# A light convolution and SwiGLU kernel: the first pair's weight conversion, fetch and loads put in another order

## The chip, the cores and the metric

The kernel runs on one core of one Trainium2 chip. The metric is the device time of one execution in microseconds (us). A few words recur: PE is TensorE, DVE is VectorE, ACT is ScalarE, POOL is GpSimd, SP is SyncE; in the traces read here VectorE, ScalarE, GpSimd and SyncE take their instructions in the order of the program, so a waiting instruction holds up all that stand behind it on its engine.

## The reference

The reference is a causal 7-tap convolution over the sequence with softmaxed taps for each of 8 heads, then a SwiGLU feed-forward with an RMS norm in front of it:

```python
def _moe_ref(x, w_gate, w_val, w_out, rms_g):          # x: 32768 x 192, d_ff 1536
    rms = np.sqrt(np.mean(x * x, axis=-1, keepdims=True) + 1e-06)
    xn = x / rms * rms_g
    g = xn @ w_gate
    silu = g * (1.0 / (1.0 + np.exp(-g)))
    val = xn @ w_val
    return (silu * val @ w_out).astype(np.float32)
```

The weights arrive as 64-bit floats and are turned into fp32 on the chip with integer operations. That conversion is what much of the change is about.

## The kernel before

The tokens are taken in 32 "pairs" of 1024. The d_ff dimension is cut into four "units". From the second pair on, a unit uses sums of weights (a fast matrix product); the first pair runs "plain" units straight from the converted weights, because the sums aren't there yet. The whole opening is a hand-made schedule: generators are stepped at fixed places, and each engine's queue gets its instructions in that order. The parts that matter (cuts marked):

```python
def convert(t, exp, mf, dst, gain=None):
    lo, hi = t[:, :, :, 0], t[:, :, :, 1]          # the two words of a 64-bit float
    nc.vector.tensor_scalar(out=exp, in0=hi, scalar1=20, ...)        # exponent field
    nc.vector.tensor_scalar(out=exp, in0=exp, scalar1=896.0, ...)    # clamp
    yield
    nc.vector.tensor_scalar(out=exp, in0=exp, scalar1=896.0, scalar2=2.0**23, op0=ALU.subtract, op1=ALU.mult)
    nc.vector.tensor_scalar(out=man, in0=hi, scalar1=0xFFFFF, ...)   # mantissa
    yield
    nc.scalar.activation(mf, man, AF.Copy, scale=2.0**-20, bias=1.0)
    # ... then DVE sign (L196), low word (L206) and gain (L211) for input weights;
    #     ACT low word, DVE sign, POOL add and product for output weights

def plain(u, side):
    ht = big.tile([P, 2, NF, T], F32, name="ht")
    n = 0
    for g in (1, 0):
        for f in range(NF):                        # six groups a unit
            bk = free[n % 4]                       # which of four pairs of PSUM banks
            n += 1
            # ... KP x 2 matmuls into bank(0, bk) and bank(1, bk)
            sg = sgs.tile([P, T], F32, name="sg")
            nc.scalar.activation(out=sg[:], in_=bank(0, bk)[:], func=AF.Silu)
            nc.vector.tensor_tensor(out=ht[:, g, f, :], in0=bank(1, bk)[:], in1=sg[:], op=ALU.mult)
            side(n)                                # everything else is stepped here

done(conv(0, True))
# ... norm, conversion of unit 0's weights, transposes
fetch(0, nc.scalar)                                # first x blocks: SyncE and ScalarE
done(cin)
load_in(2, nc.sync)
load_in(3, nc.sync)
cin = convert_in(1)
cout = convert_out()
nxt = front(1)                                     # pair 1: convolution, norm, transposes
step(nxt, 15)
for u in range(NU):
    def side(s):
        step(cin); step(cout); step(nxt, 2); step(ws)
    hts.append(plain(u, side))
    done(ws)
    ws = w_sums(u)                                 # sums of unit u's weights, on GpSimd
    done(cin)
    cin = convert_in(u + 2)
```

I number the groups of the four units 1 to 24 through the whole text; "the product" of a group is VectorE's multiplication of its SiLU and value.

Of the kernel before, what the change touches and what calls it, by code (L numbers as in the profile page):

```python
# [8 lines left out]
AF = mybir.ActivationFunctionType  # L9
ALU = mybir.AluOpType  # L10
AX = mybir.AxisListType
U32 = mybir.dt.uint32
# [3 lines left out]
def kernel(  # L16
# [10 lines left out]
    nc = tc.nc  # L27
# [26 lines left out]
    LOW, UPP = slice(0, HP), slice(HP, P)  # L54
# [66 lines left out]
    def words(w):  # L121
        return w.bitcast(U32).rearrange("r (n two) -> r n two", two=2)

    def load_in(u, q):
        cols = slice(u * NF * P, (u + 1) * NF * P)
        t = big.tile([P, 2, NF, T], F32, name="ht")
        t = t[:].rearrange("p a f t -> p (a f t)")[:, 0 : KP * NF * P * 2].bitcast(U32)
        t = raw["in", u] = t.rearrange("p (k n two) -> p k n two", k=KP, two=2)
        for w, rows in ((moe_w_gate, LOW), (moe_w_val, UPP)):
            for k in range(KP):  # L130
                q.dma_start(out=t[rows, k], in_=words(w)[k * HP : (k + 1) * HP, cols, :])

    def load_out(i, q=nc.gpsimd):
        if i >= NO:
            return
        t = outs.tile([P, T // P, D], F32, name="o_sb")
        t = t[:].rearrange("p j d -> p (j d)").bitcast(U32)
        t = raw["out", i] = t.rearrange("p (f d two) -> p f d two", f=PF, two=2)
        for f in range(PF):
            r = (i * PF + f) * P  # L140
            q.dma_start(out=t[:, f], in_=words(moe_w_out)[r : r + P, :, :])
# [14 lines left out]
        out=taps[:], in0=w_sb[:], in1=stat[:].to_broadcast([P, H, K]), op=ALU.subtract  # L156
# [7 lines left out]
        out=taps[:], in0=taps[:], in1=ssum[:].to_broadcast([P, H, K]), op=ALU.mult  # L164
    )

    def convert(t, exp, mf, dst, gain=None):





        lo, hi = t[:, :, :, 0], t[:, :, :, 1]
        nc.vector.tensor_scalar(  # L174
            out=exp, in0=hi, scalar1=20, scalar2=0x7FF,
            op0=ALU.logical_shift_right, op1=ALU.bitwise_and,
        )
        nc.vector.tensor_scalar(
            out=exp, in0=exp, scalar1=896.0, scalar2=1151.0, op0=ALU.max, op1=ALU.min
        )  # L180
        yield
        nc.vector.tensor_scalar(
            out=exp, in0=exp, scalar1=896.0, scalar2=2.0**23,
            op0=ALU.subtract, op1=ALU.mult,
        )
        man = mf.bitcast(U32)
        nc.vector.tensor_scalar(
            out=man, in0=hi, scalar1=0xFFFFF, scalar2=None, op0=ALU.bitwise_and
        )
        yield  # L190
        nc.scalar.activation(mf, man, AF.Copy, scale=2.0**-20, bias=1.0)
        if gain is None:
            low = lo.bitcast(F32)
            nc.scalar.activation(low, lo, AF.Copy, scale=2.0**-52)
        yield
        nc.vector.scalar_tensor_tensor(  # L196
            out=exp, in0=hi, scalar=0x80000000, in1=exp,
            op0=ALU.bitwise_and, op1=ALU.bitwise_or,
        )
        pw = exp.bitcast(F32)  # L200
        if gain is None:
            nc.gpsimd.tensor_tensor(out=mf, in0=mf, in1=low, op=ALU.add)
            nc.gpsimd.tensor_tensor(out=dst, in0=mf, in1=pw, op=ALU.mult)
        else:
            yield
            nc.vector.scalar_tensor_tensor(  # L206
                out=mf, in0=lo, scalar=2.0**-52, in1=mf, op0=ALU.mult, op1=ALU.add
            )
            yield
            for i in range(dst.shape[1]):  # L210
                nc.vector.scalar_tensor_tensor(  # L211
                    out=dst[:, i, :], in0=mf[:, i, :], scalar=gain[:, i : i + 1],
                    in1=pw[:, i, :], op0=ALU.mult, op1=ALU.mult,
                )
        yield
# [46 lines left out]
    def convert_in(u):  # L262
        if u >= NU:
            return
        dst = wf[u][:, 0:9, :].rearrange("p (k f) n -> p k (f n)", k=KP)
        yield from convert(raw.pop(("in", u)), exp_i[:], mf_i[:], dst, rg_sb)

    def convert_out():
        for i in range(NO):
            dst = wo_sb[:, i * PF : (i + 1) * PF, :]  # L270
            exp_o = cvt.tile([P, PF, D], U32, name="exp_o")
            mf_o = cvt.tile([P, PF, D], F32, name="mf_o")
            yield from convert(raw.pop(("out", i)), exp_o[:], mf_o[:], dst)
            load_out(i + 2)
# [5 lines left out]
    def conv(p, fast=False):  # L280


        if p >= PAIRS:
            return
        t = x_sb.pop(p)
        y = ys[p] = work.tile([P, NJ, D], F32, name="y")
        for k in range(K):
            xk = t[:, k : k + NJ, :]
            if fast and k < 3:
                for h in range(H):  # L290
                    hs = slice(h * GS, (h + 1) * GS)
                    w = taps[:, h, k : k + 1]
                    if k == 0:
                        nc.vector.tensor_scalar(
                            out=y[:, :, hs], in0=xk[:, :, hs], scalar1=w, scalar2=None,
                            op0=ALU.mult,
                        )
                    else:
                        nc.vector.scalar_tensor_tensor(
                            out=y[:, :, hs], in0=xk[:, :, hs], scalar=w, in1=y[:, :, hs],  # L300
                            op0=ALU.mult, op1=ALU.add,
                        )
                yield
                continue
            m = y if k == 0 else prods.tile([P, NJ, D], F32, name="m")
            for h in range(H):
                hs = slice(h * GS, (h + 1) * GS)
                nc.scalar.mul(m[:, :, hs], xk[:, :, hs], taps[:, h, k : k + 1])  # L308
                if h % 2:
                    yield  # L310
            if k > 0:
                nc.vector.tensor_tensor(out=y[:], in0=y[:], in1=m[:], op=ALU.add)  # L312
            yield
        load(p + 1)
# [37 lines left out]
    def place(p):  # L352




        if p >= PAIRS:
            return
        y = ys.pop(p)
        nt = work.tile([P, D // Q, Q, NJ], F32, name="nt")  # L360
        yv = y[:].rearrange("p j (c a) -> p c j a", a=Q)
        nv = nt[:].rearrange("p c b j -> p c j b")
        for c in range(D // Q):
            nc.vector.transpose(out=nv[:, c], in_=yv[:, c])  # L364
            yield
        xd = scr[p] = dram.tile([D, PT], F32, name="xd")
        to = xd[:].rearrange("(c a) (q t) -> q a c t", a=Q, q=NQ)
        for q in range(NQ):
            nc.sync.dma_start(
                out=to[q], in_=nt[q * Q : (q + 1) * Q].rearrange("p c b j -> p c (b j)")  # L370
            )
        yield
# [4 lines left out]
    def blk(i):  # L377
        return xb[:, i // KP, i % KP, :]

    def fetch(p, other=None):  # L380

        if p >= PAIRS:
            return
        xd = scr.pop(p)
        for g in (1, 0):
            for rows, q in ((LOW, nc.sync), (UPP, other or nc.sync)):
                q.dma_start(
                    out=xb[rows, g],
                    in_=xd[:, g * T : (g + 1) * T].rearrange("(k p) t -> p k t", p=HP),
                )  # L390
# [31 lines left out]
    def leftover():  # L422
        while late:
            late.pop()()

    def unit(u, side):


# [44 lines left out]

        mm(9, d, blk(B3), True)
        side(1)
        mm(12, c, cs(SS), True)
        keep("e", c)
# [127 lines left out]
    def step(it, n=1):  # L605
        for _ in range(n):
            next(it, None)

    def done(it):
        for _ in it:  # L610
            pass

    def front(p):
        yield from conv(p)
        yield from norm(p)
        yield from place(p)
# [1 line left out]


    done(conv(0, True))  # L620
    cin = convert_in(0)
    nm = norm(0, True)
    step(nm, 3)
    step(cin, 2)
    done(nm)
    step(cin)
    done(place(0))
    fetch(0, nc.scalar)
    done(cin)
    load_in(2, nc.sync)  # L630
    load_in(3, nc.sync)
    cin = convert_in(1)
    cout = convert_out()
    nxt = front(1)
    step(nxt, 15)
    hts = []
    ws = iter(())
    for u in range(NU):

        def side(s):  # L640
            step(cin)
            step(cout)
            step(nxt, 2)
            step(ws)

        hts.append(plain(u, side))
        done(ws)
        ws = w_sums(u)
        done(cin)
        cin = convert_in(u + 2)  # L650
    done(cout)
    done(nxt)

# [3 lines left out]
    for p in range(PAIRS):  # L657
# [11 lines left out]
        nxt = front(p + 2)  # L669
# [42 lines left out]
```

## Time and profile before

| | before |
|---|---|
| time, median (6 runs beside the changed kernel) | 2848.03 us (2847.11 to 2848.41) |
| TensorE's first matmul | 46.29 us |
| gaps of TensorE before units 1, 2, 3 | 5.25, 4.68, 7.96 us |
| output projection of pair 0 starts | 136.5 us |
| one later pair | 54.94 + 31.32 us of TensorE |

The lines themselves are in the prediction below. In a timeline row come the start in us, the length in us, the engine, the source line, the operation, its output and inputs with their shapes, how many instructions are merged in the row, and in brackets the idle time before it and what ended it. In the page's row of shares each engine has its busy time, its share of the span and its number of instructions.

### The profile page before, as it was taken

How to read it: one execution, taken by the hardware profiler on the slowest of the kernel's cores; microseconds unless marked ns; L12 is line 12 of the kernel's file. 1: busy time of each engine (PE TensorE's matmuls, PEld its weight loads, DVE VectorE, ACT ScalarE, POOL GpSimd, SP SyncE). 2: the span in 40 equal slices, each digit the busy share in tenths (PEclk: the TensorE clock that was granted, in tenths of full speed). 3: DMA queues.
4: the chain of work that ended last, by engine and by line, in shares of the span. 5: the costliest groups of instructions: out<-in, count | busy, mean ns of one | idle time of the engine just before them, and what ended most of it. 6: DMA issues, size and time to landing. Idle time of an engine off the chain costs nothing.

```text
span 2846.6 us, 53025 instructions
## 1 busy us (share of the span) xinstructions
PE 2777.9 (98%) x20512; PEld 2213.8 (78%) x20512; DVE 2095.7 (74%) x3188; ACT 1969.6 (69%) x4743; POOL 470.4 (17%) x409
## 2 busy tenths in 40 slices
PE   2899999999999999999999999999999999999999
PEld 1478887788887788877788877888877888877887
DVE  7677777777777777777777778777777777777754
ACT  5467777677776677776677776777766777766733
POOL 1721111111111111111111111111111111111100
PEclk9899999999999999999999999999999999999999
DMA  6212221112221112212112221122211122121110
GB/s 155 70 42 54 65 59 40 49 48 65 65 54 45 43 54 65 65 40 59 43 54 65 59 46 49 45 61 65 59 40 42 54 65 65 42 57 43 35 45 12
DMA packets 95597, 155.18 MB, mean 55 GB/s; under 512 B 6896, under 2 KB 64752, under 8 KB 91256
## 3 DMA queue, kind: packets, MB, share of 16 engines
q1 hardware_dynamic: 93856, 149.41, 20.4%
q8 instruction: 160, 2.62, 0.4%
q0 software_dynamic: 512, 1.57, 0.2%
q10 hardware_dynamic: 976, 0.82, 0.1%
q14 instruction: 93, 0.76, 0.1%
HBM read 101.44 MB, written 50.33 MB: 53 GB/s over the span
## 4 chain that ended last, share of the span: by engine, by line
PE 97%; DVE 1%; ACT 0%; DMA 0%; issue 0%; SPq 0%; DVEq 0%
PE ps L440 60%; PE ps L563 35%; PE ps L544 2%; DMA xb<-xd 0%; DVE ht L551 0%; DVE nt L364 0%; DVE y L312 0%; DMA xd<-nt 0%; DVE exp_i L196 0%; ACT sq L324 0%; DVE mf_i L206 0%; ACT sg L550 0%; DVE exp_o L174 0%; ACT y L348 0%; DVE o_sb L572 0%
## 5 line engine op out<-in xcount | busy, mean ns | idle before, releaser
L440 PE MATMUL ps<-xc,wf 64*128 64x512 f32 x4960 | 1356.3, 589 | 0.0
L440 PEld LDWEIGHTS ps<-xc,wf 64*128 64x128 f32 x4960 | 782.1, 187 | 327.9 <-issue 12.2
L563 PEld LDWEIGHTS ps<-wo_sb,ht 64*128 64x128 f32 x12288 | 1012.7, 187 | 9.5 <-DVE o_sb L572 4.8
L563 PE MATMUL ps<-wo_sb,ht 64*128 64x192 f32 x12288 | 1017.4, 323 | 0.1
L440 PE MATMUL ps<-xb,wf 64*128 64x512 f32 x2976 | 930.5, 589 | 0.0
L448 ACT COPY tp<-ps 128x512 f32<-128x512 f32 x1240 | 660.0, 588 | 300.8 <-PE ps L440 300.8
L460 ACT ACTIVATE sg<-sg 128x512 f32<-128x512 f32 x744 | 475.8, 639 | 290.0 <-DVE sg L457 290.0
L440 PEld LDWEIGHTS ps<-xb,wf 64*128 64x128 f32 x2976 | 487.6, 187 | 188.3 <-issue 6.4
L457 DVE TENSOR_TENSOR sg<-ps,tp 128x512 f32<-128x512 f32 x620 | 425.1, 686 | 212.0 <-ACT tp L448 210.4
L312 DVE TENSOR_TENSOR y<-y,m 128x1536 f32<-128x1536 f32 x190 | 334.8, 1762 | 298.1 <-ACT m L308 297.7
L308 ACT ACTIVATE m<-x_sb,taps 128x192 f32<-128x192 f32 x1520 | 532.5, 441 | 6.8 <-DMA x_sb<-in_x_dram 6.1
L463 DVE TENSOR_TENSOR ht<-ht,sg 128x512 f32<-128x512 f32 x744 | 484.5, 683 | 0.0
L457 DVE TENSOR_TENSOR ht<-ps,tp 128x512 f32<-128x512 f32 x620 | 422.6, 682 | 0.0
L472 POOL TENSOR_TENSOR tp<-tp,sg 128x512 f32<-128x512 f32 x124 | 179.7, 1449 | 1209.8 <-ACT tp L448 1165.1
L336 POOL TENSOR_SCALAR r<-ss 128x8 f32<-128x8 f32 x32 | 10.5, 327 | 1063.7 <-ACT sq L324 1037.0
L572 DVE TENSOR_TENSOR o_sb<-ps,o_sb 128x192 f32<-128x192 f32 (+1 forms) x192 | 75.7, 420 | 115.5 <-ACT o_sb L571 113.4
L472 POOL TENSOR_TENSOR tp<-tp,ht 128x512 f32<-128x512 f32 x124 | 157.6, 1271 | 0.0
L348 ACT ACTIVATE y<-y,r 128x192 f32<-128x192 f32 x252 | 94.0, 445 | 83.2 <-POOL r L339 83.2
L457 DVE TENSOR_TENSOR sg<-tp,ps 128x512 f32<-128x512 f32 x124 | 85.3, 688 | 85.8 <-ACT tp L448 64.3
L544 PE MATMUL ps<-xb,wf 64*128 64x512 f32 x288 | 72.3, 663 | 64.2 <-DMA xb<-xd 46.3
L571 ACT COPY o_sb<-ps 128x192 f32<-128x192 f32 (+1 forms) x192 | 67.0, 364 | 88.6 <-PE ps L563 88.2
L324 ACT ACTIVATE sq<-y 128x192 f32<-128x192 f32 x252 | 91.6, 363 | 50.5 <-DVE y L312 43.6
(52 smaller groups left out, 779.4 us busy)
## 6 DMA issues: line engine op xcount, KB each, us to landing
xb<-xd SPq DMA_DIRECT2D x126, 384.0 KB, 6.4
x_sb<-in_x_dram SPq DMA_DIRECT2D x24, 1344.0 KB, 5.8
xd<-nt SPq DMA_DIRECT2D x128, 192.0 KB, 3.3
out_dram<-o_sb SPq DMA_DIRECT2D x64, 384.0 KB, 2.6
x_sb<-in_x_dram SPq DMA_DIRECT2D x8, 1176.0 KB, 9.0
ht<-in_moe_w_gate_dram SPq DMA_DIRECT2D x12, 192.0 KB, 9.1
ht<-in_moe_w_val_dram SPq DMA_DIRECT2D x12, 192.0 KB, 5.9
o_sb<-in_moe_w_out_dram POOLq DMA_DIRECT2D x8, 192.0 KB, 2.8
```

The source lines that it names most:

```text
L308: nc.scalar.mul(m[:, :, hs], xk[:, :, hs], taps[:, h, k : k + 1])
L312: nc.vector.tensor_tensor(out=y[:], in0=y[:], in1=m[:], op=ALU.add)
L324: nc.scalar.activation(out=sq[:], in_=y[:, j, :], func=AF.Square, accum_out=ss[:, j : j + 1])
L348: nc.scalar.mul(y[:, j, :], y[:, j, :], r[:, j : j + 1])
L440: nc.tensor.matmul(out=bank(h, bk)[:], lhsT=wf[u][rows, at[i], :], rhs=rhs, start=first, stop=True, skip_group_check=True,)
L448: nc.scalar.copy(out=t[:], in_=bank(h, bk)[:])
L457: nc.vector.tensor_tensor(out=dst, in0=in0, in1=in1, op=op)
L460: nc.scalar.activation(out=og[o][:], in_=og[o][:], func=AF.Silu)
L463: nc.vector.tensor_tensor(out=ov[o], in0=ov[o], in1=og[o][:], op=ALU.mult)
L472: nc.gpsimd.tensor_tensor(out=t[:], in0=sb["a", h][:], in1=o3, op=ALU.add)
L544: nc.tensor.matmul(out=bank(h, bk)[:], lhsT=wf[u][HALF[h], k * NF + f, :], rhs=xb[HALF[h], g, k, :], start=(k == 0), stop=(k == KP - 1), s ...
L563: nc.tensor.matmul(out=bank(h, bk)[:, w : w + D], lhsT=hts[f // NF][HALF[h], g, f % NF, j * P : (j + 1) * P], rhs=wo_sb[HALF[h], f, :], st ...
```

## The change

It means to remove the three gaps of TensorE in the first pair. Five things move: one of VectorE's exponent steps becomes a ScalarE copy; the first fetch of x is issued by SyncE alone, so that ScalarE needn't wait in front of it; the third unit's weights are loaded before the fetch; the second unit's weights are converted before the first unit instead of beside it; and the later conversions are stepped at chosen groups.

```diff
         nc.vector.tensor_scalar(
             out=exp, in0=exp, scalar1=896.0, scalar2=1151.0, op0=ALU.max, op1=ALU.min
         )
-        yield
-        nc.vector.tensor_scalar(
-            out=exp, in0=exp, scalar1=896.0, scalar2=2.0**23,
-            op0=ALU.subtract, op1=ALU.mult,
-        )
 ... (mantissa as before)
         yield
+        nc.scalar.activation(exp, exp, AF.Copy, scale=2.0**23, bias=-896.0 * 2.0**23)
         nc.scalar.activation(mf, man, AF.Copy, scale=2.0**-20, bias=1.0)
 ...
     done(conv(0, True))
-    cin = convert_in(0)
+    load_in(2, nc.sync)
     nm = norm(0, True)
     step(nm, 3)
-    step(cin, 2)
+    cin = convert_in(0)
+    step(cin)
     done(nm)
     step(cin)
     done(place(0))
-    fetch(0, nc.scalar)
+    fetch(0)
+    load_in(3, nc.sync)
+    nxt = front(1)
+    step(nxt, 5)
     done(cin)
-    load_in(2, nc.sync)
-    load_in(3, nc.sync)
     cin = convert_in(1)
+    step(cin)
+    step(nxt, 5)
+    step(cin)
+    step(nxt, 5)
+    done(cin)
 ... (inputs(): convert_in(2), then convert_in(3))
         def side(s):
-            step(cin)
+            n = 6 * u + s
+            if n <= 13 and n % 2 or 14 <= n <= 16:
+                step(cin)
             step(cout)
             step(nxt, 2)
             step(ws)
```

More of the change, by code (lines that the diff above doesn't have):

```diff
@@ L173, in convert @@
         lo, hi = t[:, :, :, 0], t[:, :, :, 1]
+        man = mf.bitcast(U32)
         nc.vector.tensor_scalar(
@@ L180, in convert @@
         )
-        yield
-        nc.vector.tensor_scalar(
-            out=exp, in0=exp, scalar1=896.0, scalar2=2.0**23,
-            op0=ALU.subtract, op1=ALU.mult,
-        )
-        man = mf.bitcast(U32)
         nc.vector.tensor_scalar(
@@ L378, in blk, with fetch @@
         return xb[:, i // KP, i % KP, :]
-    def fetch(p, other=None):
+    def fetch(p):
         if p >= PAIRS:
@@ L385, in fetch @@
         for g in (1, 0):
-            for rows, q in ((LOW, nc.sync), (UPP, other or nc.sync)):
-                q.dma_start(
+            for rows in (LOW, UPP):
+                nc.sync.dma_start(
                     out=xb[rows, g],
@@ L627, with inputs @@
     done(place(0))
-    fetch(0, nc.scalar)
+    fetch(0)
+    load_in(3, nc.sync)
+    nxt = front(1)
+    step(nxt, 5)
     done(cin)
-    load_in(2, nc.sync)
-    load_in(3, nc.sync)
     cin = convert_in(1)
+    step(cin)
[3 more added lines that the diff above has]
+    done(cin)
+    def inputs():
+        yield from convert_in(2)
+        yield from convert_in(3)
+    cin = inputs()
     cout = convert_out()
-    nxt = front(1)
-    step(nxt, 15)
     hts = []
@@ L648 @@
         ws = w_sums(u)
-        done(cin)
-        cin = convert_in(u + 2)
+    done(cin)
     done(cout)
```

## The prediction

> **What bounds the kernel now.** I first read the page's engine shares and its chain that ended last.
>
> ```profile
> PE 2777.9 (98%) x20512; PEld 2213.8 (78%) x20512; DVE 2095.7 (74%) x3188; ACT 1969.6 (69%) x4743; POOL 470.4 (17%) x409
> PE 97%; DVE 1%; ACT 0%; DMA 0%; issue 0%; SPq 0%; DVEq 0%
> ```
>
> TensorE (PE) carries the end. The same chain in order of time shows a strict rhythm from 136.49 us on, of which these are the first pieces:
>
> ```profile
> 118.24 18.25 PE ps L544 x72
> 136.49 31.27 PE ps L563 x384
> 167.76 54.93 PE ps L440 x256
> 222.69 31.40 PE ps L563 x383
> ```
>
> Line 563 is the output projection, line 440 the later pairs' units, line 544 the four plain units of the first pair, the only part that the change touches. Everything after 136.5 us hangs on TensorE alone, so a shift of that instant should come out one for one in the time, and nothing else should. TensorE's own timeline shows what those 136.5 us hold:
>
> ```profile
> 46.29 18.38 PE L544 MATMUL ps<-xb,wf 64*128 64x512 f32 x72 [46.29 <-DMA xb<-xd]
> 69.92 18.51 PE L544 MATMUL ps<-xb,wf 64*128 64x512 f32 x72 [5.25 <-DVE wf L211]
> 93.11 17.16 PE L544 MATMUL ps<-xb,wf 64*128 64x512 f32 x72 [4.68 <-ACT sq L324]
> 118.24 18.25 PE L544 MATMUL ps<-xb,wf 64*128 64x512 f32 x72 [7.96 <-DVE wf L211]
> ```
>
> At full clock 256 matmul records of line 440 take 54.93 us, 0.2146 us each, so a unit of 72 needs 15.45 us and four need 61.8. They take 136.5 - 46.3 = 90.2: 17.9 us of gaps (5.25 + 4.68 + 7.96), and 72.3 busy - 61.8 = 10.5 us of running slowly. The stretches show where the slowness is; after the stretch and its length stand the busy time of PE, PEld, DVE, ACT and POOL with the number of instructions, then the granted clock, the DMA share and GB/s:
>
> ```profile
> 69.90:75.40 5.50, 5.49 (x14) 2.58 (x16) 1.47 (x4) 0.00 (x0) 0.00 (x0) 0.50 0.01 3
> 75.40:88.40 13.00, 13.00 (x61) 5.86 (x58) 12.29 (x16) 9.83 (x22) 8.08 (x9) 0.99 0.18 64
> ```
>
> After a gap the clock is half for 5.5 us: 14 records in place of about 25. Gap and slow start together are the prize: 17.9 + 10.5 = 28.4 us, 1.0% of the kernel. Hence no outcome reaches 2%.
>
> **What the Trainium skill says.** (1) "TensorE: Matmul & The Clock Gate", Part 1, What's actually happening: the clock is halved after an idle window of about 3.4 us, and comes back after about 3.4 us of work. The trace agrees: all three gaps are above 4.6 us and each is followed by slow records (2.9, 3.1, 1.7 and 2.8 us above 15.45 in the four units, the first included). (2) "DMA: Bandwidth & Descriptors", Issuing engines are not separate DMA queues: a second issuing engine saves only its sequencer's issue time. Here ScalarE pays far more than it saves, because it stands in order behind the wait for xd:
>
> ```profile
> 31.71 1.15 ACT L191 ACTIVATE mf_i<-mf_i 128x1152 f32<-128x1152 uint32 x1
> 39.94 1.31 ACTq L387 DMA_DIRECT2D xb<-xd  x2
> 41.37 2.87 ACT L308 ACTIVATE y<-x_sb,taps 128x192 f32<-128x192 f32 x8 [8.51 <-issue]
> ```
>
> (3) "ScalarE: Activation LUTs", What ACT_TABLE_LOAD costs: an ACTIVATE with immediate scale and bias takes 186 ns + 0.833 ns an element; for 1152 elements 1.146 us, and the row above has 1.15. The new exponent copy has that form, so 1.15 us for input weights and 0.51 for output weights (384 elements). (4) "SBUF — State Buffer", Who interferes with whom: a VectorE instruction with two SBUF inputs contends with a GpSimd instruction that reads SBUF. The trace agrees: line 206 takes 1.33 us with GpSimd idle, 1.84 with it at work.
>
> ```profile
> 35.89 1.33 DVE L206 SCALAR_TENSOR_TENSOR mf_i<-ht,mf_i 128x1152 f32<-128x1152 uint32 x1
> 63.61 1.84 DVE L206 SCALAR_TENSOR_TENSOR mf_i<-ht,mf_i 128x1152 f32<-128x1152 uint32 x1
> ```
>
> **The change part by part.**
>
> *Exponent factor to ScalarE.* VectorE loses four instructions of 0.76 us and six of 0.36, 5.2 us; ScalarE gains 4 x 1.15 + 6 x 0.51 = 7.7 us. A conversion also has fewer steps: five instead of six for input weights, three instead of four for output weights. ScalarE was 5 tenths busy in this stretch, so the trade is right, and it lies beside TensorE.
>
> *Fetch by SyncE alone.* The first two transfers were issued together at 39.93 and TensorE got both at 46.15. Now the second follows one issue later (0.61 to 0.79 us), but the first group no longer shares the engines with the second group and the weights. The next pair's fetch, SyncE alone, has two issues from 128.77 and its second landing about 5.3 to 5.9 us later. I take the start of TensorE as 45.7 instead of 46.3. The real gain is ScalarE's freedom: pair 1's first products start when the transposes end, 34.8, not at 41.4.
>
> *Third weights sooner.* The pair-1 input is read until about 27.5 us, the DMA engines are then empty until 35.8. Six weight transfers of 192 KB (1.18 MB at 215 GB/s, 5.5 us) fit between, to about 33, so the xd writes are not pushed.
>
> *Second unit's weights ahead.* VectorE, by its in-order rows: transposes to 34.8, first conversion to 38.9, three opening instructions of the second to 41.1, the sum of tap 1 to 42.8; then it must wait for ScalarE's tap 2 (ScalarE: three taps of 2.8 us from 34.8, with two conversion copies of 1.1 between, to 45.3), sums to 47.0, then 1.26 + 1.3 + 1.7 to 51.3. The second unit's weights are ready at 51.3, the first group of matmuls ends about 51.2 (5.5 us, half clock), and unit 1 is due only at 45.7 + 18.4 = 64.1. The 5.25 us gap goes.
>
> *The rest of the pair.* I walked the 24 groups through ScalarE, VectorE and GpSimd in program order, by the durations of the trace's rows less the 0.08 us overlap of successive rows. Groups end every 2.575 us from 51.2. Four pairs of PSUM banks rotate, so the product of group n must be done when group n + 3 ends. Third weights: steps at groups 1, 3, 5, 7, 9; I get the last at 76.3, due at 79.3. The 4.68 us gap goes too. Fourth weights: steps at groups 11, 13, 14, 15, 16, due at 94.8. Here I find a wait. The norm's r is made on GpSimd at group 13, in order behind its backlog: from 68.5 us the second output conversion's product 1.05, three weight loads 3.6, unit 0's fifteen sums and three negations 11, two more output conversions 4.1, r 2.4, and 0.4 of waits, 22.7, so r at about 91.3. The kernel before needed 20.5 us for nearly that list (81.47 to 102.1) and there too ScalarE waited for it:
>
> ```profile
> 102.16 0.80 ACT L348 ACTIVATE y<-y,r 128x192 f32<-128x192 f32 x2 [4.15 <-POOL r L339]
> ```
>
> From r to the fourth weights, in order: two y 0.75, SiLU 0.6, [output conversion's three copies 1.25, four y 1.4, SiLU 0.6], product 0.65, line 206 1.6, small mask 0.5, transpose 0.55, product 0.65, three of line 211 1.9: 10.4. Ready at 101.8. Unit 2's last group starts at 93.4 rather than 92.2 (its bank's product of group 14 is late) and ends at 96.0; so TensorE idles about 5.8 us, and unit 3 starts at half clock, 15.45 + 2.7 = 18.15. End of the units: 101.8 + 18.2 = 120.0. Check by sums: 45.7 + 61.8 + 2.9 + 2.7 slow + 7.0 idle = 120.1. The output conversions end near 107, before the projection. Saving 136.5 - 120.1 = 16.4 us.
>
> **The rivals.** (a) *TensorE never waits again after its start*: 45.7 + 61.8 + 2.9 = 110.4, saving 26.1, 2822. For: the designer hurried the steps at 14 to 16, as if fitted to a deadline, and VectorE has only about 50 us of work in 65. Against: GpSimd's 95% busy stretch from 90 to 110 us before, which the change doesn't shorten. If GpSimd gave r with no queue, the walk has r at 87, fourth weights at 97.5, no cold restart, and 2825. (b) *My walk*, 2832. (c) *The third weights too arrive late, or r at 95*: with line 312's sums at 2.0 instead of 1.76 and lines 196, 206, 211 at their contended 1.9, 1.8, 2.0, some 4 us more, 2836; a second cold restart would give 2838. (d) *The start gets later*, by weights in front of the xd writes or the lone queue: 1 us for each us. (e) *The time saved is given back later*: nothing in the chain after 136.5 speaks for it, since each pair takes 54.94 + 31.32 us of TensorE.
>
> **Range and chances.** I take 2831, a little under the walk's 2832, as (a) pulls harder than (c). Eight in ten: 2824 (r nearly in time) to 2837. Two per cent faster would be 2791, out of reach of the 28.4 us to be had; slower by 57 us would need the pattern after 136 us to break.
>
> **What would show each step.** TensorE's four rows of line 544: the first at 45 to 46.3; the second and third joined to it without a gap; before the fourth a gap of 4 to 7 us whose releaser is line 211, with the clock half for the next 5 us; the projection from 118 to 122. ScalarE's first L348 of pair 1 after a wait for r of 3 to 5 us, r near 91. ScalarE's 8.5 us issue gap gone. I am wrong if the fourth row has no gap (GpSimd or VectorE has more slack than I walked), if a gap stands before unit 2, or if the time differs from the shift of the projection's start by over 1 us.

## The result, and the profile after

The changed kernel took 2837.4 us (2836.44 to 2838.37, 6 runs) against 2848.03: a gain of 10.6 us, 0.4%. The ratio is 0.9963 with a 95% interval of 0.995 to 0.9976. A ratio is the mean time of one kernel's fast runs over that of the other's of the same rounds, so not quite the ratio of the medians quoted. The direction and "within 2%" were right; the median lies 0.4 us above the range (two of the six runs lie inside it) and 6.4 above the predicted 2831.

The page's engine shares and its chain by engine, after:

```profile
PE 2776.3 (98%) x20512; PEld 2206.5 (78%) x20512; DVE 2090.6 (74%) x3178; ACT 1975.9 (70%) x4753; POOL 465.3 (16%) x409
PE 97%; DVE 1%; POOL 1%; DMA 0%; issue 0%; ACT 0%; SPq 0%; DVEq 0%; POOLq 0%
```

VectorE has ten instructions fewer and ScalarE ten more, as the diff says. TensorE still carries the end, but GpSimd has appeared in the chain. In order of time (start, length, what) the chain after reads:

```profile
93.54 1.69 POOL r L335
...
103.52 1.80 DVE wf L207 x3
106.76 1.03 DVE nt L360 x2
108.36 16.65 PE ps L540 x69
125.53 30.87 PE ps L559 x377
```

The projection (line 559, 563 before) starts at 125.5 us instead of 136.5: 11.0 us sooner, and the time fell by 10.6. So nothing was given back later; the whole question is why 125.5 and not 120.1. TensorE's timeline after, to be held against the four rows in the prediction:

```profile
44.39 22.84 PE L540 MATMUL ps<-xb,wf 64*128 64x512 f32 x86 [44.39 <-DMA xb<-xd]
68.61 13.15 PE L540 MATMUL ps<-xb,wf 64*128 64x512 f32 x60 [1.38 <-DVE ht L547]
83.60 16.56 PE L540 MATMUL ps<-xb,wf 64*128 64x512 f32 x70 [1.84 <-DVE ht L547]
104.18 1.40 PE L540 MATMUL ps<-xb,wf 64*128 64x512 f32 x2 [4.02 <-DVE wf L207]
108.36 16.91 PE L540 MATMUL ps<-xb,wf 64*128 64x512 f32 x69 [2.78 <-DVE ht L547]
```

The rows no longer break at the units. A group has 12 records. The first row has 86, that is unit 0 and 14 more: it breaks two records into group 8. The next breaks at 146, two records into group 13, and the fourth at 218, two records into group 19. Each time the two records are the first half of the bank pair, which ScalarE's SiLU frees, and the other half waits for line 547, VectorE's product. The gaps sum to 10.0 us instead of 17.9, TensorE's busy time to 71.2 instead of 72.3. The clock stretches show the cost of the last two gaps (PEclk is the third number from the end):

```profile
84.00:96.00 12.00, 11.95 (x56) 5.24 (x53) 4.91 (x9) 6.39 (x19) 11.51 (x17) 1.00 0.22 66
106.00:109.00 3.00, 0.64 (x2) 0.51 (x4) 3.00 (x7) 1.86 (x4) 2.76 (x7) 0.50 0.00 0
109.00:112.00 3.00, 3.00 (x10) 1.21 (x8) 2.66 (x4) 0.00 (x0) 2.44 (x4) 0.56 0.00 0
```

After the short gap at 83.6 the clock is full; after 4.02 + 2.78 us with two records between, it is half. ScalarE's rows for pair 1's first products, and for its wait for the norm's r, answer to those of before:

```profile
34.96 2.88 ACT L304 ACTIVATE y<-x_sb,taps 128x192 f32<-128x192 f32 x8 [0.96 <-ACT mf_i L187]
95.26 0.80 ACT L344 ACTIVATE y<-y,r 128x192 f32<-128x192 f32 x2 [5.49 <-POOL r L335]
```

The 8.51 us that ScalarE stood in front of the fetch are gone; the wait for r is 5.5 us, at 95.2.

### The profile page after: what moved, and what is told of

Read it like the earlier page. It is cut to its first block, busy times and chain, and to the rows that moved or that the text cites. A ratio compares the mean times of both kernels' runs of the same rounds, so it can differ in the third digit from the quotient of the medians.

```text
span 2835.1 us, 53033 instructions
## 1 busy us (share of the span) xinstructions
PE 2776.3 (98%) x20512; PEld 2206.5 (78%) x20512; DVE 2090.6 (74%) x3178; ACT 1975.9 (70%) x4753; POOL 465.3 (16%) x409
## 4 chain that ended last, share of the span: by engine, by line
PE 97%; DVE 1%; POOL 1%; DMA 0%; issue 0%; ACT 0%; SPq 0%; DVEq 0%; POOLq 0%
PE ps L436 60%; PE ps L559 35%; PE ps L540 1%; POOL wf L228 0%; DVE nt L360 0%; DVE ht L547 0%; DMA xb<-xd 0%; DMA xd<-nt 0%; DVE wf L207 0%; POOL wf L231 0%; ACT y L344 0%; POOL o_sb L141 0%; POOL wo_sb L199 0%; DVE mf_i L202 0%; POOL r L335 0%
## 5 line engine op out<-in xcount | busy, mean ns | idle before, releaser
L453 DVE TENSOR_TENSOR sg<-tp,ps 128x512 f32<-128x512 f32 x124 | 85.3, 688 | 84.8 <-ACT tp L444 64.3
L540 PE MATMUL ps<-xb,wf 64*128 64x512 f32 x288 | 71.2, 626 | 54.5 <-DMA xb<-xd 44.4
```

Of the source, the lines that this page charges most:

```text
L453: nc.vector.tensor_tensor(out=dst, in0=in0, in1=in1, op=op)
L540: nc.tensor.matmul(out=bank(h, bk)[:], lhsT=wf[u][HALF[h], k * NF + f, :], rhs=xb[HALF[h], g, k, :], start=(k == 0), stop=(k == KP - 1), s ...
```

## The experiments

Theory A, after this reading: two waits stand between the walk and the measurement. The bank counter of the plain units restarts at 0 in every unit, so with six groups and four pairs of banks the first two groups of a unit reuse the banks of the groups *two* back, not four (the prediction said four); and r is late on GpSimd, which makes the fourth weights late. Rival B: VectorE's total backlog paces everything, and these waits only show where it surfaces. The runs came on different chips and aren't compared by tenths across them; each is held to the runs of the kernel before in its own rounds, and mechanisms are read from traces. The 95% intervals of the ratios are some 0.0015 to either side, so among the variants the medians, whose runs scatter by 0.5 to 3.6 us, are the finer but less safe measure.

**e1_rotate**: the changed kernel with a running bank counter.

```diff
-                bk = free[n % 4]
+                bk = free[(2 * NF * u + n) % 4]
```

> Changed kernel, with the plain units' bank counter running on over the four units (it restarted at 0 in each). Theory A (bank reuse at a unit's start waits for the product only two groups back): the gaps of 1.38 us at 68.6 and 1.84 us at 83.6 in TensorE's row of line 540 vanish, and unit 3 no longer waits at 108.4 for the product of group 17: it flows from its weights (about 104) at half clock and ends near 122 instead of 125.4. Because the fourth weights come from r on GpSimd and not from TensorE, the gap before unit 3 grows by what the early gaps lose. Time 2833 to 2835. Rival B (VectorE's backlog as a whole paces the products): the gaps only move to other groups and the time stays at 2837 +- 1.

Measured: 2832.93 us (before 2849.03; ratio 0.9944, interval 0.9929 to 0.9959), just under the expected band. TensorE's timeline of this run:

```profile
44.18 47.72 PE L540 MATMUL ps<-xb,wf 64*128 64x512 f32 x204 [44.18 <-DMA xb<-xd]
96.24 5.53 PE L540 MATMUL ps<-xb,wf 64*128 64x512 f32 x12 [4.34 <-ACT sg L546]
103.82 17.42 PE L540 MATMUL ps<-xb,wf 64*128 64x512 f32 x72 [2.04 <-DVE wf L207]
```

17 groups (204 records) run without a gap, and every gap left stems from r or the fourth weights. Group 18 now starts late (96.24) for the reason that the walk gave: the SiLU and the product of group 14, which held its banks, come behind r. Unit 3 starts with its weights at 103.8 and ends at 121.2 instead of 125.3. The restart was a real wait, worth about 4 us.

**e2_sums_late**: GpSimd's weight sums are emitted from group 14 on, behind r.

```diff
-    ws = iter(())
+    ws = all_sums()                 # w_sums(0), w_sums(1), ... in one generator
 ...
-            step(ws)
+            if n >= 14:
+                step(ws)
 ...
-        done(ws)
-        ws = w_sums(u)
```

> Changed kernel, with GpSimd's weight sums of units 0 to 2 emitted from group 14 on, so behind the norm's r. Theory A (GpSimd's backlog makes r late and r the fourth weights): r ends at 88 to 91 us instead of 95.2, ScalarE's wait for r falls from 5.5 us to 0 to 2, line 207's third-to-last row for unit 3 starts 4 to 6 us sooner, unit 3 likewise; time 2831 to 2834. Also VectorE's lines 192, 202, 207 lose their contended durations before group 13 (1.83 back to 1.35). Rival B (VectorE's own amount of work sets the fourth weights): they come less than 1.5 us sooner, time 2836 to 2838.

Measured: 2832.15 us (ratio 0.9942, 0.9926 to 0.9959). r was ready at 90.0 instead of 95.2, ScalarE waited 1.6 us for it instead of 5.5, and the fourth weights began at 97.8 instead of 103.4. The third weights' last instructions (VectorE's line 207), first in the changed kernel, then in this one, show the contention with GpSimd as well:

```profile
75.97 2.56 DVE L207 SCALAR_TENSOR_TENSOR wf<-mf_i,rg_sb,exp_i 128x384 f32<-128x384 f32 x3
```

```profile
75.66 1.67 DVE L207 SCALAR_TENSOR_TENSOR wf<-mf_i,rg_sb,exp_i 128x384 f32<-128x384 f32 x3
97.82 2.05 DVE L207 SCALAR_TENSOR_TENSOR wf<-mf_i,rg_sb,exp_i 128x384 f32<-128x384 f32 x3
```

With GpSimd idle the three take 1.67 us, with sums running 2.56. Rival B falls: VectorE has the same instructions here, and the fourth weights came 5.6 us sooner. In the changed kernel VectorE even stood idle for 6.4 us (90.2 to 96.6) until ScalarE had r; it was not the pace there. The shorter contended durations are a second effect of the same edit (VectorE was busy 27.9 of the 30 us from 60 to 90 us in the changed kernel, 26.3 here), which this run doesn't separate from r.

**e3_both**: both edits.

> Both edits. Theory A: no gap before units 1 and 2, unit 3 starts at its weights near 98, ends near 115 to 117; time 2826 to 2830, more than the sum of the two single gains, as each alone leaves the other wait at unit 3's start. Rival B: 2835 to 2838.

Measured: 2827.49 us (ratio 0.9926, 0.9911 to 0.9941). The expected time holds; that the gain would be more than the sum does not. Against the kernel before the gains are 10.6 us for the change, 16.1 with the counter, 16.9 with the late sums and 21.5 with both: 10.9 more than the change, where the single ones give 5.5 and 6.3. What is left in TensorE's timeline:

```profile
44.29 51.54 PE L540 MATMUL ps<-xb,wf 64*128 64x512 f32 x216 [44.29 <-DMA xb<-xd]
98.69 17.42 PE L540 MATMUL ps<-xb,wf 64*128 64x512 f32 x72 [2.87 <-DVE wf L207]
```

Three units without a gap, then one gap before unit 3.

**e4_fetch_two**: the changed kernel with the upper half of the first fetch issued by ScalarE again.

```diff
-            for rows in (LOW, UPP):
-                nc.sync.dma_start(
+            for rows, q in ((LOW, nc.sync), (UPP, other or nc.sync)):
+                q.dma_start(
 ...
-    fetch(0)
+    fetch(0, nc.scalar)
```

> Changed kernel, with the first fetch on SyncE and ScalarE again. If the lone queue brought the earlier start of TensorE (44.4 instead of 46.3), it goes back to 46.0 to 46.5; ScalarE stands idle from 34 to 41.4 in front of the fetch, the second unit's weights come some 6 us later (near 58) but still before they are due at 64; TensorE's later waits shift by 2 us or grow by up to 3. Time 2839 to 2842. If the start moved for another reason (the third weights no longer behind the fetch), it stays at 44.4 and the time within 1 us of 2837.

Measured: 2844.03 us (ratio 0.9984, 0.9969 to 0.9999), 2 us above the expected band. The start went back:

```profile
46.72 15.43 PE L540 MATMUL ps<-xb,wf 64*128 64x512 f32 x62 [46.72 <-DMA xb<-xd]
```

So the earlier start (44.4) belongs to the lone queue, not to the earlier third weights, which this run keeps. From the first fetch's issue to the first matmul it took 6.5 us with two queues (40.18 to 46.72) and 4.4 with one (39.99 to 44.39). The kept traces point to the reason. These lines show what each queue had moved from 40 us to the first matmul (packets, MB, share of the DMA engines' time), first in the kernel before (q10 is ScalarE's queue, q1 SyncE's), then in the changed one:

```profile
q10 hardware_dynamic: 365, 0.71, 46.6%
q1 hardware_dynamic: 208, 0.39, 25.3%
```

```profile
q1 hardware_dynamic: 332, 0.65, 57.6%
```

The first matmul needs only SyncE's first transfer, 0.39 MB. With two queues ScalarE's transfers moved 0.71 MB beside it; with one, 0.26 MB moved beside it. The rate was about the same (from 41.30 to 44.39 us 219 GB/s before, 209 after), so the DMA engines were not slower; the transfer that TensorE waits for shared the engines with less. Little of this start lasts: group 2's first record begins at 50.5 us in the changed kernel and 50.8 here, unit 0's last at 63.4 and 64.7. The part's worth lies with ScalarE. It idled 7.4 us in front of the fetch, and r came at 101.7, 6.5 us later than in the changed kernel: the loss passes through r undiminished.

**e5_expo_vector**: the changed kernel with the exponent factor on VectorE again.

```diff
+        nc.vector.tensor_scalar(
+            out=exp, in0=exp, scalar1=896.0, scalar2=2.0**23,
+            op0=ALU.subtract, op1=ALU.mult,
+        )
 ... (mantissa)
-        nc.scalar.activation(exp, exp, AF.Copy, scale=2.0**23, bias=-896.0 * 2.0**23)
```

> Changed kernel with the exponent factor back on VectorE (the steps kept as they are). If that part helps by VectorE's load: VectorE has 5.2 us more work, of it 3 to 4 us between groups 1 and 16, ScalarE 7.7 us less; ScalarE's r wait begins sooner, but r itself hangs on GpSimd. Time 2837 to 2840. If ScalarE is as tight as VectorE here, nothing or a gain: 2835 to 2837.

Measured: 2840.84 us (2840.09 to 2842.2; ratio 0.9975, 0.996 to 0.999), 0.8 us above the first case. r came at 97.0, 1.8 us later, and there were five gaps behind products instead of three (the largest 2.55 us at 85.3). The part helps by unloading VectorE.

**e6_load_late**: the changed kernel with the third weights loaded behind the fetch.

```diff
     done(conv(0, True))
-    load_in(2, nc.sync)
 ...
     fetch(0)
+    load_in(2, nc.sync)
     load_in(3, nc.sync)
```

> Changed kernel with the third weights loaded behind the fetch again. TensorE's start stays at 44.2 to 44.9 (the lone queue's work, as the run with two fetch queues says). The third weights land about 54 instead of 33; VectorE wants them at 52.2 in group 1's side, so it stands 1 to 3 us there; r is late by as much or less: 2837 to 2840. If the early load moved nothing but idle transfer time: 2837 +- 1.

Measured: 2841.97 us (ratio 0.9978, 0.9961 to 0.9994), 2 us above the expected band. TensorE's start stayed (44.74). The waits of this run, who waited for whom, in total us, times and the longest:

```profile
DVE exp_i L175 <- DMA ht<-in_moe_w_val_dram: 3.8, 1, 3.8
```

VectorE stood 3.8 us for the third weights in group 1's side, where I had said 1 to 3; TensorE then had a gap of 3.5 us before unit 1, and r came at 99.7, 4.4 us later than in the changed kernel. So the early load did more than fill idle transfer time: VectorE wants these weights, in program order, beside group 1.

**e7_second_behind**: the second unit's weights converted beside unit 0 (steps at groups 1 to 5, then 6 to 10, then 11 to 16).

```diff
-    cin = convert_in(1)
-    step(cin)
-    step(nxt, 5)
-    step(cin)
-    step(nxt, 5)
-    done(cin)
+    step(nxt, 10)
     def inputs():
+        yield from convert_in(1)
         yield from convert_in(2)
 ...
-            if n <= 13 and n % 2 or 14 <= n <= 16:
+            if n <= 13 or 15 <= n <= 16:
                 step(cin)
```

> Changed kernel with the second unit's weights converted beside the first unit again (steps at groups 1 to 5, the third unit's at 6 to 10, the fourth's at 11 to 16). Unit 1's weights come near 65 to 68 instead of 51.6, TensorE has a gap of 2 to 4 us before unit 1, maybe with a half clock after; VectorE has 4.3 us more work before group 16. Time 2840 to 2845. If the second conversion only fills time that is free in either place: 2837 to 2839.

Measured: 2843.9 us (2841.73 to 2845.28; ratio 0.9985, 0.997 to 0.9999). Unit 1 started at 69.05 after a gap of 3.16 us, and group 13's second half came 4.62 us late behind a product. In this profile all the opening was 1.2 us late from its first transfers on (TensorE's start 45.94), so a part of the loss is scatter.

**e8_sooner**: e3_both, and the fourth weights' steps put before the wait for r, the output conversion paused.

```diff
-            if n <= 13 and n % 2 or 14 <= n <= 16:
-                step(cin)
-            step(cout)
+            if n <= 9 and n % 2 or 10 <= n <= 12:
+                step(cin)
+            if n == 13:
+                step(cin, 2)
+            if n < 11 or n > 16:
+                step(cout)
```

> The kernel of both edits (bank counter running on, weight sums from group 14), and further: the fourth weights' steps at groups 10 to 13, before the wait for r, and the output conversion paused over groups 11 to 16. Theory A says that only r stood before the fourth weights: they come before 92, no gap stands in TensorE's row of line 540 any more, the projection starts at 109 to 112; time 2821 to 2824. Rival B (VectorE's work is the pace): a gap of 2 us or more before unit 3 or a stall in the groups before; 2825 to 2829.

Measured: 2827.79 us (ratio 0.9929, 0.9914 to 0.9944): no better than e3_both, though the projection started where I had said, at 110.9, in spite of a late fetch (start at 46.40). The gain was given back afterwards:

```profile
93.62 17.86 PE L540 MATMUL ps<-xb,wf 64*128 64x512 f32 x81 [0.35 <-DVE ht L547]
...
125.51 19.53 PE L559 MATMUL ps<-wo_sb,ht 64*128 64x192 f32 x236 [1.58 <-POOL wo_sb L199]
```

The wait before unit 3 is gone; in its place the projection waits at 125.5 for the last output weights, which GpSimd multiplies, and ScalarE waited 5.8 us for pair 2's r, which came at 149.0. GpSimd's queue ran without a pause from 90 to 149, and all that the pause had put off lay in it. The time fits the numbers of rival B, but not its signs: no gap of 2 us stands in the four units.

**e9_before_fetch**: the kernel before, with the first fetch on SyncE alone.

```diff
-    fetch(0, nc.scalar)
+    fetch(0)
```

> The kernel before with only the first fetch on SyncE alone. If the start of TensorE is the lone queue's, it goes to 44.2 to 45.0 here too, and ScalarE starts pair 1's products near 34.8 instead of 41.4; but the waits for the second unit's weights (VectorE, in order behind the sums and ScalarE's copies of its own group) stay, so of the 6.6 us that the same part is worth in the changed kernel only 2 to 4 are seen: 2844 to 2846. If the part pays alone as in company: 2841 to 2842.

Measured: 2845.64 us against 2848.58 (ratio 0.9992, 0.9977 to 1.0007). TensorE started at 44.63, the gaps 4.49, 4.81 and 6.54 us remained, and the projection's records began at 133.6. The part alone shows 2.9 us; taken from the changed kernel it costs 6.6. The interval includes 1, so only the trace's start and gaps are firm here.

**e10_before_rotate**: the kernel before, with the running bank counter.

```diff
-                bk = free[n % 4]
+                bk = free[(2 * NF * u + n) % 4]
```

> The kernel before with only the bank counter running on over the units. Before, every unit waited for its weights (69.9, 118.2) or for ScalarE (93.1), not for a product, so the bank reuse should not have shown: 2847 to 2849; at most the unit at 93.1 comes sooner by 1 to 2 us. If the bank restart was a wait of the kernel before too: 2844 or less.

Measured: 2847.19 us against 2848.58 (ratio 0.9997, 0.998 to 1.0013): no difference to be told. The units still wait for their weights. That holds for unit 2 too, though the profile names ScalarE's line 324 as its releaser and I had taken it so: its first record, at 93.11 us before, comes 0.75 us after VectorE's line 211 began on its weights (92.36), just as unit 1's does (69.17 to 69.92), and here it is 0.76 us (91.49 to 92.25). The bank restart was in the kernel before too, but behind longer waits.

**e11_sums_split**: e8_sooner with unit 0's sums at groups 7, 8, 11 and 12.

```diff
-            if n >= 14:
+            if n in (7, 8, 11, 12) or 14 <= n <= 21:
                 step(ws)
```

> As e8_sooner, but unit 0's weight sums at groups 7, 8, 11 and 12, where GpSimd stood idle before r, and nothing of unit 3's sums before its matmuls are done. e8_sooner gave back its gain because GpSimd's queue then ran full from 90 to 149: the projection waited for the last output weights at 125.5, pair 2's r came at 149. With 12 us of sums taken out of that stretch the last output weights come near 114 to 118 and pair 2's r near 146 or before, so no gap stands in the projection and none in pair 1's first unit. Theory A: 2822 to 2825. If GpSimd's backlog is not what gave it back: 2827 to 2828 again.

Measured: 2825.01 us (2824.61 to 2825.19; ratio 0.9918, 0.9904 to 0.9933), at the upper end of the expected 2822 to 2825, and the fastest of all.

```profile
44.44 39.92 PE L540 MATMUL ps<-xb,wf 64*128 64x512 f32 x170 [44.44 <-DMA xb<-xd]
86.31 27.28 PE L540 MATMUL ps<-xb,wf 64*128 64x512 f32 x117 [1.96 <-DVE ht L547]
...
113.50 31.24 PE L559 MATMUL ps<-wo_sb,ht 64*128 64x192 f32 x378
```

One gap of 1.96 us is left, behind a product on VectorE. Short as it is, the clock fell to half 1.1 us after it:

```profile
87.40:90.80 3.40, 3.40 (x12) 1.48 (x10) 2.38 (x3) 2.88 (x12) 3.22 (x6) 0.50 0.00 0
```

The projection starts later than in e8_sooner (113.0 against 110.9) but no longer waits: the last output weights ended at 119.5, pair 2's r at 145.4, so the loss of e8_sooner was GpSimd's backlog.

## Why the prediction was right or wrong

By its own signs the prediction was wrong in two places: a gap stands at unit 2's start (83.6 us, two records into it), and the projection began at 125.5 us instead of 118 to 122. The gap before unit 3 behind its weights (4.02 us, 4 to 7 expected) and the time following the projection's start within 1 us came out. From the predicted 120.0 to 125.5 the sum is: fourth weights for unit 3 at 104.2 instead of 101.8, 2.4 us; unit 3's wait for a bank, 4.2 us; its run from there 17.2 instead of 18.2, 1.0 us back.

- **Only the instant of the projection counts.** Right. It moved by 11.0 us, the time by 10.6. The same held for the variants in which GpSimd stayed on time; e8_sooner shows the limit of the sentence.
- **TensorE's start at 45.7.** The direction was right and the size too small: 44.4. e4_fetch_two and e9_before_fetch show that it is the lone queue, and the bytes moved by each queue bear out the reason given, that the first blocks share the engines with less. That ScalarE's freedom is "the real gain" was right too.
- **The gap before unit 1 goes.** Right for the weights (VectorE's last instructions for them ended at 51.7; I had 51.3). It was replaced by 1.38 us in group 8, which the walk lacked.
- **The third weights in time at 76.3.** Off by 2.2 us: they ended at 78.5. Two sums of VectorE and line 207 ran at contended durations (line 207's three took 2.56 us; I had 1.7). They were still in time.
- **"Four pairs of PSUM banks rotate, so the product of group n must be done when group n + 3 ends."** This is the step that failed. It holds within a unit only; the counter starts anew at each unit, so the first two groups of units 1 to 3 (7 and 8, 13 and 14, 19 and 20) need the product two groups back and had half the slack. Three of the four gaps in TensorE's timeline are this wait. In the last one it fell on the worst place: after the fourth weights were there (104.2) unit 3 stood until 108.4 for group 17's product, which lay in VectorE's order behind the weights themselves, the first three instructions of an output conversion and two transposes. e1_rotate undoes exactly this and puts the end of the units at 121.2; the walk had 120.1. So about 4 of the 5.5 us are this one line of code, which I had read and not applied.
- **r at 91.3.** The mechanism was right, the size 3.9 us short: it was ready at 95.2. The mis-sized term is "unit 0's fifteen sums and three negations 11": they took 13.5 us. The kernel before's own trace would have said 12.8 (65.5 to 96.3); the 20.5 us stretch that I checked against holds only twelve of the fifteen sums, and these with the negations took 11.3. The waits in the list were 1.6 us, not 0.4, and the list began at 69.2, not 68.5. (The list as written adds up to 22.55, not 22.7; that is too small to matter.) These rows of the changed kernel's GpSimd show both:

```profile
71.23 5.07 POOL L228 TENSOR_TENSOR wf<-wf 128x128 f32<-128x128 f32 x7
79.16 0.99 POOL L199 TENSOR_TENSOR wo_sb<-mf_o,exp_o 128x384 f32<-128x384 f32 x1 [1.57 <-DVE exp_o L192]
81.39 2.39 POOL L228 TENSOR_TENSOR wf<-wf 128x128 f32<-128x128 f32 x2
```

  Seven sums took 0.72 us each, and two took 1.2 each while VectorE's sum of line 308 (81.2 to 82.9) ran. VectorE's busy share alone doesn't set this: five sums from 106.9 on took 0.47 each while VectorE was busy all the time, but with transposes and products.
- **10.4 us from r to the fourth weights.** Right: 95.2 to 105.3. But TensorE needs only the first of the three line-207 instructions to start, at 104.2, so this term was a little on the safe side.
- **One restart at half clock, before unit 3.** Right: stretches at 0.50 and 0.56. From its weights unit 3 took 17.4 us in e1_rotate and e3_both; I had 18.15. My first point on the skill said that the trace agrees with about 3.4 us of work before the full clock comes back; the kernel before took 5.7, 3.0 and 5.1 us after its three gaps.
- **Rival (a), no more waits (2822).** It failed for the kernel as changed. e11_sums_split comes to within 3 us of it by re-ordering alone. My reason for leaning below the walk, that a hurried schedule at groups 14 to 16 looked fitted to a deadline, was a guess about the author and pulled the wrong way.
- **The parts.** Taken away one at a time, the fetch cost 6.6 us, the exponent factor 3.4, the early third load 4.6 and the conversion ahead 6.5 (by medians; the last partly scatter). They sum to 21.1 of a gain of 10.6: so their worths overlap, and several run through the same r (6.5 us later in e4_fetch_two, 4.4 in e6_load_late). That each needs the others isn't shown: the fetch alone, in e9_before_fetch, may be worth 2.9 us.

What stays open: how the last 1.96 us in e11_sums_split would be won, how much of e7_second_behind's loss is scatter, and when a gap halves the clock (see the last section).

## What to carry to other kernels

When TensorE waits at block boundaries, write out for each group which earlier group last held its PSUM bank; a counter that restarts in every block halves the slack where it is needed most, and shows only once the longer waits are gone (e1_rotate against e10_before_rotate). Look for small results that come from a busy helper engine in order (here r behind GpSimd's sums): one 2 us instruction can hold the whole pipe by its place in the queue. After moving work out of such a queue's way, check that it doesn't come due all at once later.

## What the Trainium skill lacked or had wrong

- "DMA: Bandwidth & Descriptors", Issuing engines are not separate DMA queues: it says that the transfers of several issuing engines interleave on the same DMA engines and that a second one saves only the time to issue, and the traces agree (0.71 MB of ScalarE's transfers moved beside SyncE's first 0.39 MB). It doesn't say that this can delay the transfer that is waited for. Here TensorE started 6.4 to 6.5 us after the first issue from two queues (before, e4_fetch_two, e10_before_rotate) and 4.4 to 4.7 us after it from one (nine runs); a tenth, e8_sooner, had 5.7.
- "SBUF — State Buffer", Who interferes with whom: it names who contends but gives no size for such a mix. Here VectorE's three line-207 instructions took 1.67 us alone and 2.56 beside GpSimd's sums, and a GpSimd sum took from 0.5 (five in 2.34 us, VectorE at 0.3 busy) to 1.2 us (two in 2.39 us, beside VectorE's line 308).
- "TensorE: Matmul & The Clock Gate", Part 1, What's actually happening: its table puts the half clock after at least one idle window of about 3.4 us. Here the length of a gap didn't decide. Gaps of 1.38 and 1.84 us (the changed kernel) and of 2.55 us (e5_expo_vector, at 85.3) left the granted clock at 1.00; gaps of 4.02 and 2.78 us with two records between left it at 0.50, and e11_sums_split's single gap of 1.96 us was followed by 3.4 us at 0.50. What decides isn't shown.
